# Spectral mixing and a gated bilinear layer: earlier direct weights at the block change, normalisation on two engines, and three low parts and a product group in another order

## The chip, the cores and the metric

The kernel runs on one core of a Trainium2 chip. The metric is the device time of one execution in microseconds (us); 727.72 us is the median of three runs of the kernel before, which lie between 727.48 and 728.47. TensorE is the matrix engine, VectorE (DVE), ScalarE (ACT) and GpSimd (POOL) are the other computing engines, and SyncE (SP) issues transfers. Each engine works through its own instructions in the order in which the program gives them; an instruction that waits holds everything behind it on the same engine.

## What is computed

The reference is a transformer-like block on 2048 tokens of 640 channels, in 32-bit floats:

```python
def _layernorm(x, axis=-1, eps=1e-5): ...
def _A_ref(x, w_r, w_i):                       # a filter in the frequency domain
    X = jnp.fft.rfft2(x, axes=(-2, -1))
    X = X * (w_r + 1j * w_i)
    return jnp.fft.irfft2(X, s=(S, D), axes=(-2, -1))
def _B_ref(x, w_gate, w_up, w_down):           # bilinear gate, F = 1728
    h = jnp.einsum("bsd,df->bsf", x, w_gate) * jnp.einsum("bsd,df->bsf", x, w_up)
    return jnp.einsum("bsf,fd->bsd", h, w_down)
h = x + _A_ref(_layernorm(x), w_r, w_i)
h2 = h + _B_ref(_layernorm(h), w_gate, w_up, w_down)
```

## The kernel before

**Stages.** The tokens are 16 tiles of 128 rows (tile t holds tokens t, t + 16, ...). First come the first layer norm and the forward transform (to about 115 us), then the inverse transform tile by tile: `id_mm`, `unfold` and `is1_mm` make the result of tile t and `acc` (L510) adds it to the rows `X[t]`. Tiles 8 to 15 are then written out to DRAM (the spill, L686), since their place in SBUF is wanted for something else. After that the bilinear layer runs in two blocks of eight tiles: block 0 (tiles 0 to 7), then block 1 (tiles 8 to 15).

**High and low parts.** The matrix products are done in a reduced 32-bit format. To keep accuracy, an operand is split into a high part (a copy in the reduced format, on ScalarE) and a low part (the operand less the high part, a subtraction on VectorE or GpSimd), and a product is three matmuls: high by high, high by low, low by high. `high_of` is L739, `low_of` L743; for weights it is `split_in` (L465 and L466) and `prep` (L706 to L723).

**The bilinear layer.** The 1728 gate columns are 14 pieces. Pieces 12 and 13 are done first in each block and directly (`p == 6` in the loop at the end: `gu` and `gate_parts`), with the direct weights that `load_direct` brings; pieces 0 to 11 are the chunks of a seven-product Strassen scheme (`strassen(c, ...)`, two chunks for each of the six steps p). A chunk computes into three PSUM banks, `p11`, `acc_a` and `p53`, out of four. In one chunk, in the order of the program: a product group into `acc_a`, copied by ScalarE (`p1`, L973); one into `p11`; a further one on `acc_a`, copied as `u2` (L987); one into `p53`, copied as `m5` (L995); one more on `acc_a`, added to `m5` on VectorE (L1002); one more on `p53`, to which `u2` is added (L1005). Then `h[0]` multiplies (L808), makes the high part on ScalarE and returns a function, `rest`, that makes the low part on VectorE. A last group on `acc_a` follows, and `h[1]` does the same with it. Between these stand the slots `at(0)` to `at(6)`, where work listed in `side` is put in; they come in the order 0, 1, 2, 3, 6, 4, 5.

**Down projection.** The gated results of a step are multiplied by the down weights during the next step, either as whole products (`down`, with `acc`) or, behind a "mixed" step, as 16 small stages (`mixed_down`, with the row additions at L917) that `tick` weaves between the matmul triples of the first chunk. Such a chunk is `woven`; `tick` also takes one function from the list `pending` (`flush(1)`). Steps 1 to 4 are mixed in block 0, steps 0 to 4 in block 1; step 5 (chunks 10 and 11) is not, but its chunk 10 is woven, as the step before it was mixed. In mixed chunks `rest` is an empty function.

**The block change.** In chunk 11 of block 0, `bring_back` (L731) loads the eight spilled tiles into the rows' old place; its first load waits for TensorE's last use of that place, in chunk 10. `load_direct` loads the direct weights of the next block: the 640 columns of `wlast` into a work buffer, and two halves of 640 columns into the staging tile `stage`. All eleven loads go to SyncE's queue. At slot 1 the weights are split (ScalarE L465, GpSimd L466) and the next raw weights are loaded. At slots 3, 6 and 5 `low` normalises tiles 8 to 15 (L527: scale and shift per row), on ScalarE. Block 1 then opens (`p == 6`): for each of the eight tiles, four transposes on TensorE (L539), copies on ScalarE (L549, L553) and subtractions on VectorE (L557), with a group of down products of block 0 (12 matmuls and one `acc`) after each tile but the first.

**The opening of block 0.** In the loop over the inverse transform, at t = 13 (`NT - 3`), new PSUM banks are opened and `gu(NC - 1, 0)` runs ahead of the products of tile 13. Later, in `p == 6` of block 0, `late()` is the low part of piece 12 (L658); it stands behind `t_rest` (eight subtractions), the t34 split and the low parts of the weights on VectorE.

Of the kernel before, what the change touches and what calls it, by code (L numbers as in the profile page):

```python
# [14 lines left out]
OP = mybir.AluOpType  # L15
# [31 lines left out]
def tile_spectral_glu(ctx: ExitStack, tc: tile.TileContext, x, wf, wgu, wlast, wdown, wdlast,  # L47
# [51 lines left out]
    def home(tag, shape, name, dt=F32):  # L99
        return keep.tile(shape, dt, tag=tag, name=name)  # L100
# [401 lines left out]
    def is1_mm(t):  # L502
        ps = PY[t] = pair("y")
        for b in range(2):
            mmx(ps[:, b, 0:320], cit, YT[t][:, 320 * b:320 * b + 320], True, True)
# [16 lines left out]
            SC[t] = r[:, i:i + 1], b[:, i:i + 1]  # L522
        return fs, cs

    def normalise(t, z):
        Z[t] = z
        act(z, X[t], AF.Identity, bias=SC[t][1], scale=SC[t][0])  # L527

    PT = {}
# [135 lines left out]
    for t in range(NT):  # L665
        for k in tside[t]:
            turn_mm(k)
        if t + 2 < NT:
            unfold(t + 2, dside[t], tside[t])
        else:  # L670
            for k in tside[t]:
                turn_hi(k)
                turn_lo(k)
        if t + 3 < NT:
            id_mm(t + 3)
        for f in aside[t]:
            f()
        if t == NT - 3:
            ht = home("qm", [P, 8192], "ht", F32R)
            hts, t3 = cut(ht, 0, 3, 2, 2, 512), cut(ht, 6144, 2, 2, 512)  # L680
            banks("a", "pglu")
            gu(NC - 1, 0)
        is1_mm(t)
        acc(t, PY[t], total[:, t:t + 1] if t < 8 else None)
        if t >= 8:
            nc.sync.dma_start(spill[t - 8], X[t])  # L686
        if t == NT - 2:
            late = gate_parts(NC - 1, 0, 0)
# [251 lines left out]
    def strassen(c, blk, h, ahead, downs, side, fine=()):  # L940
        wa, ws = W[c]
        fine = list(fine)

        def some(n):
            for _ in range(n):
                if downs:
                    downs.pop(0)()
                    pop(2)

        def at(n):  # L950
            if c == 1 and blk == 0:
                pop(5)
            for f in side.get(n, ()):
                f()

        def tick():
            if fine:
                fine.pop(0)()
                flush(1)

        b11, b21, b22 = ([operand(sb, k + i) for i in range(2)] for sb, k in ((0, 0), (0, 2), (1, 2)))
        t1, t2 = ([(TJ["12"][:, 0, m, k], TJ["12"][:, 1, m, k]) for k in range(2)] for m in range(2))
        t4 = [operand(1, k) for k in range(2)]
        b5 = [operand(sb, 4) for sb in range(2)]
        p11, acc_a, p53 = single(), single(), single()

        def product(o, w, a, ms, extra=(), start=True, tick=tick):
            triple(o, [(w, a + P * i, m) for i, m in enumerate(ms)] + list(extra), start, tick)

        woven = bool(fine)  # L970
        product(acc_a, wa, 384, b11, tick=None)
        p1, u2, m5 = (wk([P, 512], n) for n in ("p1", "u2", "m5"))
        act(p1, acc_a, AF.Copy)  # L973
        at(0)
        if not woven:
            flush(1)
        product(p11, wa, 0, b21, [(wa, 256, b5[0])])
        if ahead and not woven:
            ahead[0]()
            flush(2)  # L980
            ahead[1]()
            flush()
        if not woven:
            tt(p1, p11, p1, op=OP.add)
        at(1)
        product(acc_a, ws, 0, t2, start=False)
        act(u2, acc_a, AF.Copy)  # L987
        flush()
        if woven:
            tt(p1, p11, p1, op=OP.add)  # L990
        if ahead and woven:
            ahead[0]()
            ahead[1]()
        product(p53, ws, 256, t1, [(wa, 896, b5[1])])
        act(m5, p53, AF.Copy)  # L995
        if ahead and woven:
            ahead[2]()
            ahead[3]()
        some(2)
        at(2)  # L1000
        product(acc_a, ws, 640, [(t3[:, k, 0], t3[:, k, 1]) for k in range(2)], start=False)
        tt(m5, acc_a, m5, op=OP.add)  # L1002
        some(1)
        product(p53, ws, 896, b22, [(ws, 512, b5[1])], start=False)
        tt(p53, p53, u2, op=OP.add)  # L1005
        rest = h[0](p53, m5)
        at(3)
        some(2)
        rest()
        if ahead and not woven:  # L1010
            ahead[2]()
            ahead[3]()
        product(acc_a, wa, 640, t4, [(wa, 896, b5[0])], start=False)
        while fine:
            tick()
        some(1)
        at(6)
        rest = h[1](acc_a, p1)
        at(4)
        some(1)  # L1020
        rest()
        some(8)
        at(5)
# [5 lines left out]
    for n, (blk, p) in enumerate(steps):  # L1029
        if p == 6:  # L1030
            s13, s12 = count % 3, (count + 1) % 3
            if blk == 0:
                load_raw(0)
                copies, sums, high, low = prep(0, blk, nc.vector)
                TJ["12"] = home("qr", [P, 2, 2, 2, 512], "t12", F32R)
                t1s = [t12(j) for j in range(4)]
                for j in range(4):
                    t1s[j][0]()
                copies()
                t1s[0][1]()  # L1040
                late()
                t1s[1][1]()
                t1s[2][1]()
                fifth((5, 6, 7))
                t1s[3][1]()
                late = gate_parts(NC - 2, 0, s12)
                sums()
                high()
                for j in range(4):
                    t_rest(j)  # L1050
                hi, lo = t34(0)
                hi()
                low()
                lo()
                late()
                gu(NC - 1, 1)
                wdn = load_d(p)
                gate_parts(NC - 1, 1, s13)()
            else:
                copies, sums, high, low = prep(0, blk)  # L1060
                js = [4, 5, 6, 7, 0, 1, 2, 3]
                for j in range(8):
                    transp(8 + j)
                    if j % 4 == 3:
                        fifth(range(5 + j, 9 + j))
                    if j >= 1:
                        down(*prev, js[j - 1], True)
                    if j == 3:
                        copies()
                        sums()  # L1070
                high()
                low()
                down(*prev, js[7], True)
                gu(NC - 1, 0)
                gate_parts(NC - 1, 0, s13)()
                gu(NC - 2, 0)
                TJ["12"] = home("qr", [P, 2, 2, 2, 512], "t12", F32R)
                t1s = [t12(j) for j in range(4)]
                late = gate_parts(NC - 2, 0, s12)
                for j in range(4):  # L1080
                    t1s[j][0]()
                    t_rest(j)
                late()
                gu(NC - 1, 1)
                for j in range(4):
                    t1s[j][1]()
                wdn = load_d(p)
                late = gate_parts(NC - 1, 1, s13)
                hi, lo = t34(0)
                hi()  # L1090
                late()
                lo()
            gu(NC - 2, 1)
            gate_parts(NC - 2, 1, s12)()
            first_wd = wdn
            prev = (blk, 6, [(2 * k, 2 * k + 1) for k in (s12, s13)])
            count += 2
            load_raw(1)
            if blk == 0:
                fs, cs = scale_shift(range(8, 16), None)  # L1100
                fill.extend(fs + cs)
            continue
# [15 lines left out]
        for ci in range(2):  # L1118
# [11 lines left out]
            elif ci == 0:  # L1130
                side[3] = [lambda wdn=wdn: issue(wdn)]
            if c == 11 and blk == 0:
                bring_back()
                dj = load_direct(1, [wk([P, D], "draw"), stage[:, 0:640], stage[:, 640:1280]])
                side[1] = [lambda: issue(dj[0]), lambda: issue(dj[1]), lambda: load_raw(0)]

                def low(ks):
                    for k in ks:
                        if k == 0:
                            TJ["z"] = home("qr", [P, 6, D], "zt")  # L1140
                        normalise(8 + k, TJ["z"][:, k] if k < 6 else wk([P, D], "z"))

                side[3] = [lambda: low(range(4))]
                side[6] = [lambda: low((4, 5))]
                side[5] = [lambda: low((6, 7))]
            strassen(c, blk, hs[ci], ahead, downs if ci == 0 else [], side, fine if ci == 0 else ())
            count += 1
        prev = (blk, p, units)
# [134 lines left out]
```

## Time and profile before

| | |
|---|---|
| median of three runs | 727.72 us |
| profiled execution, its own time | 726.67 us |
| its span in the profile | 724.9 us |
| mean granted TensorE clock | 0.99 |
| TensorE busy in 423.0 to 429.4 us | 0.00 of 6.40 us |
| idle time of TensorE that ends at L987, VectorE's L658, L496 | 6.6, 1.2, 1.1 us |

A line of the timeline reads: start, length (both us), engine, source line, operation, what it writes and reads, shape, count, and in brackets how long the engine had been idle and whose work ended that. Where a line merges several instructions, the length goes from the first's start to the last's end. PE is TensorE's matmul row, PEld its weight loads, which run beside the matmuls. L82 is the helper that all matmuls of the later stages go through, so those are told apart by tile names: `e` are the chunk's banks, `y` the banks of the down products.

### The profile page before, as it was taken

The page shows a single profiled execution, that of the slowest core. Times are in us where ns is not written, and L with a number is a line of the kernel's source. Part 1 is how long each engine was busy: PE and PEld are TensorE (multiplying, and loading weights), DVE is VectorE, ACT ScalarE, POOL GpSimd, SP SyncE. Part 2 cuts the span into 40 slices and gives each one's busy share as a digit, 9 for nine tenths or more (in the row PEclk, how much of TensorE's full clock was granted, in tenths as well). Part 3 has the DMA queues.
Part 4 walks back from the last instruction along what each step waited for, and adds up shares of the span by engine and source line. Part 5 has one row for each costly group of instructions (what it writes and reads, how often), then busy time and mean ns, then how long its engine had stood idle before and what let it go on. Part 6 is the DMA issues. An engine that isn't in the chain of part 4 may idle for free.

```text
span 724.9 us, 10120 instructions
## 1 busy us (share of the span) xinstructions
PE 694.0 (96%) x3784; PEld 607.1 (84%) x3784; DVE 477.9 (66%) x839; ACT 305.5 (42%) x574; POOL 367.0 (51%) x342
## 2 busy tenths in 40 slices
PE   7999998999999999999999967999999999999998
PEld 6788997987878898888888846989888888888887
DVE  7968887897968446666666615565565757565654
ACT  4756666365533323433334227252434252433320
POOL 3301114332155585959596621219678686868610
PEclk9999999999999999999999989999999999999999
DMA  9405765002321212121111061320030302020203
GB/s 337 166 1 174 233 213 168 1 20 81 118 74 37 72 37 73 38 73 37 58 51 38 36 234 38 128 90 26 14 108 0 110 1 103 6 79 32 72 1 146
DMA packets 23234, 60.30 MB, mean 83 GB/s; under 512 B 2577, under 2 KB 7185, under 8 KB 23185
## 3 DMA queue, kind: packets, MB, share of 16 engines
q1 hardware_dynamic: 22608, 57.94, 23.2%
q0 software_dynamic: 288, 1.48, 0.6%
q8 instruction: 30, 0.49, 0.3%
q10 hardware_dynamic: 288, 0.23, 0.1%
q14 instruction: 20, 0.16, 0.1%
HBM read 51.78 MB, written 7.86 MB: 82 GB/s over the span
## 4 chain that ended last, share of the span: by engine, by line
PE 77%; DVE 12%; issue 4%; DMA 4%; ACT 2%; POOL 0%; SPq 0%; DVEq 0%; POOLq 0%; ACTq 0%
PE e L82 41%; PE y L82 24%; PE re L82 2%; PE im L82 2%; PE u L343 2%; PE eo L82 2%; DMA raw<-in_wgu_dram 2%; DVE fold L193 1%; DVE fold L198 1%; PE im L393 1%; PE im L392 1%; PE ir L384 1%; DVE ex L743 1%; DMA x<-in_x_dram 1%; DVE xb L917 1%
## 5 line engine op out<-in xcount | busy, mean ns | idle before, releaser
L82 PE MATMUL e<-xt,wst 128*128 128x512 f32 x864 | 220.4, 393 | 1.3 <-DVE ht L658 1.2
L82 PEld LDWEIGHTS e<-xt,wst 128*128 128x128 f32 x864 | 158.6, 189 | 29.8 <-DVE ht L658 1.6
L82 PE MATMUL y<-wd,ht 128*128 128x320 f32 x880 | 152.4, 312 | 2.4 <-DVE x L510 1.0
L82 PEld LDWEIGHTS y<-wd,ht 128*128 128x128 f32 x880 | 139.9, 190 | 14.9 <-DVE x L510 1.3
L707 POOL TENSOR_TENSOR wst<-raw,wst 128x1024 fp32r<-128x1024 f32 x24 | 57.6, 2402 | 96.9 <-ACT wst L706 96.6
L82 PE MATMUL e<-t,wst 128*128 128x512 f32 x288 | 74.1, 391 | 0.0
L723 POOL TENSOR_TENSOR wst<-raw,wst 128x896 fp32r<-128x896 f32 (+1 forms) x46 | 65.1, 1436 | 9.7 <-ACT wst L718 9.7
L739 ACT ACTIVATE ht<-e 128x512 fp32r<-128x512 f32 x48 | 27.6, 596 | 92.9 <-DVE e L808 47.2
L917 DVE TENSOR_TENSOR xb<-y,xb 128x640 f32<-128x640 f32 x60 | 49.4, 824 | 26.0 <-PE y L82 24.2
L82 PEld LDWEIGHTS e<-t,wst 128*128 128x128 f32 x288 | 52.6, 188 | 8.6
L917 DVE TENSOR_TENSOR x<-y,x 128x640 f32<-128x640 f32 x48 | 39.5, 824 | 20.9 <-PE y L82 20.0
L1002 DVE TENSOR_TENSOR m<-e,m 128x512 f32<-128x512 f32 x24 | 16.5, 687 | 54.7 <-PE e L82 54.6
L743 DVE TENSOR_TENSOR ht<-e,ht 128x512 fp32r<-128x512 f32 x48 | 33.1, 689 | 23.1 <-ACT ht L739 22.6
L82 PE MATMUL e<-ht,wst 128*128 128x512 f32 x144 | 39.8, 403 | 6.6 <-ACT u L987 6.6
L718 ACT ACTIVATE wst<-raw 128x896 fp32r<-128x896 f32 (+1 forms) x48 | 30.1, 677 | 32.2 <-POOL raw L712 31.4
L82 PE MATMUL y<-ex,ht 128*128 128x320 f32 x216 | 43.4, 309 | 0.0
L82 PE MATMUL e<-xt,wdir 128*128 128x512 f32 x180 | 41.9, 392 | 1.1 <-DVE q L496 1.1
L466 POOL TENSOR_TENSOR wd<-draw,wd 128x640 fp32r<-128x640 f32 x10 | 16.3, 1653 | 49.6 <-ACT wd L465 49.6
L510 DVE TENSOR_TENSOR x<-y,x 128x640 f32<-128x640 f32 x32 | 26.2, 820 | 21.7 <-PE y L82 21.7
L82 PEld LDWEIGHTS e<-xt,wdir 128*128 128x128 f32 x180 | 33.4, 188 | 8.3 <-ACT xt L549 1.3
L411 POOL CAST qr<-bits 1x128 fp32r<-1x128 f32 x16 | 4.5, 280 | 68.0 <-DVE qr L408 68.0
L82 PEld LDWEIGHTS y<-ex,ht 128*128 128x128 f32 x216 | 36.2, 188 | 3.2
(212 smaller groups left out, 1302.8 us busy)
## 6 DMA issues: line engine op xcount, KB each, us to landing
raw<-in_wgu_dram SPq DMA_DIRECT2D x24, 640.0 KB, 3.9
wts<-in_wf_dram SPq DMA_DIRECT2D x16, 644.0 KB, 4.0
draw<-in_wdown_dram SPq DMA_DIRECT2D x24, 320.0 KB, 4.6
x<-in_x_dram SPq DMA_DIRECT2D x16, 320.5 KB, 5.9
bits<-in_mm_dram SPq DMA_DIRECT2D x32, 128.0 KB, 3.9
sp<-x SPq DMA_DIRECT2D x8, 320.0 KB, 2.1
xb<-sp SPq DMA_DIRECT2D x8, 320.0 KB, 5.3
out_dram<-x SPq DMA_DIRECT2D x8, 320.0 KB, 2.2
```

The costliest lines, as they stand in the source:

```text
L82: nc.tensor.matmul(o, l, r, start=start, stop=stop, skip_group_check=True)
L193: lambda: nc.vector.scalar_tensor_tensor(view(f, 320, [[161, 2], [1, 161]]), view(XP[t], 0, [[320, 2], [1, 161]]), SC[t][1], view(XP[t], 6 ...
L343: nc.tensor.matmul(ps[h][:, 0:NQ], WM[g][0][:, h], T[g][:, h], start=True, stop=True)
L466: los.append(lambda r=r, a=a, b=b: engine.tensor_tensor(w[:, 1, a:b], r, f32(w[:, 0, a:b]), op=OP.subtract))
L510: tt(xv, ps[:, :, 0:320], xv, op=OP.add)
L707: nc.gpsimd.tensor_tensor(wa[:, 1], stage[:, 0:1024], f32(wa[:, 0]), op=OP.subtract)
L718: act(ws[:, 0, o:o + b - a], stage[:, a:b], AF.Copy)
L723: ptt(ws[:, 1, o:o + b - a], stage[:, a:b], f32(ws[:, 0, o:o + b - a]), op=OP.subtract)
L739: act(unit(u)[0], src, AF.Copy)
L743: engine.tensor_tensor(lo, src, f32(hi), op=OP.subtract)
L917: tt(xv, PQ[q][:, :, 0:320], xv, op=OP.add)
L1002: tt(m5, acc_a, m5, op=OP.add)
```

## The change

Five edits. At the block change the three weight loads are issued ahead of the eight row loads; tiles 8 to 11 are normalised on ScalarE at slot 2 (before: slot 3), tiles 12 and 13 on VectorE at slot 3 and tiles 14 and 15 on VectorE at slot 6. In woven chunks `rest` of `h[0]` is put into `pending`, so that it comes out behind the next stage of `mixed_down`. At t = 13 the products and the addition of tile 13 come ahead of the new banks and `gu(NC - 1, 0)`. In the opening of block 0 `late()` comes ahead of `t_rest`.

```diff
-    def normalise(t, z):
+    def normalise(t, z, vector=False):
         Z[t] = z
+        if vector:
+            nc.vector.tensor_scalar(z, X[t], SC[t][0], SC[t][1], op0=OP.mult, op1=OP.add)
+            return
         act(z, X[t], AF.Identity, bias=SC[t][1], scale=SC[t][0])
...
         if t == NT - 3:
+            is1_mm(t)
+            acc(t, PY[t])
             ht = home("qm", [P, 8192], "ht", F32R)
             hts, t3 = cut(ht, 0, 3, 2, 2, 512), cut(ht, 6144, 2, 2, 512)
             banks("a", "pglu")
             gu(NC - 1, 0)
-        is1_mm(t)
-        acc(t, PY[t], total[:, t:t + 1] if t < 8 else None)
+        if t != NT - 3:
+            is1_mm(t)
+            acc(t, PY[t], total[:, t:t + 1] if t < 8 else None)
...
         some(2)
-        rest()
+        if woven:
+            pending.append(rest)
+        else:
+            rest()
...
                 high()
+                late()
                 for j in range(4):
                     t_rest(j)
                 hi, lo = t34(0)
                 hi()
                 low()
                 lo()
-                late()
                 gu(NC - 1, 1)
...
             if c == 11 and blk == 0:
+                dj = load_direct(1, [wk([P, D], "draw"), stage[:, 0:640], stage[:, 640:1280]])
                 bring_back()
-                dj = load_direct(1, [wk([P, D], "draw"), stage[:, 0:640], stage[:, 640:1280]])
                 side[1] = [lambda: issue(dj[0]), lambda: issue(dj[1]), lambda: load_raw(0)]
...
-                        normalise(8 + k, TJ["z"][:, k] if k < 6 else wk([P, D], "z"))
-
-                side[3] = [lambda: low(range(4))]
-                side[6] = [lambda: low((4, 5))]
-                side[5] = [lambda: low((6, 7))]
+                        normalise(8 + k, TJ["z"][:, k] if k < 6 else wk([P, D], "z"), k > 3)
+
+                side[2] = [lambda: low(range(4))]
+                side[3] = [lambda: low((4, 5))]
+                side[6] = [lambda: low((6, 7))]
```

## The prediction

> **What bounds the kernel now.** I read the page first, then the table of waits of TensorE, then the timeline around the waits that the change could touch, and the windows for the granted clock.
>
> ```profile
> span 724.9 us, 10120 instructions
> PE 694.0 (96%) x3784; PEld 607.1 (84%) x3784; DVE 477.9 (66%) x839; ACT 305.5 (42%) x574; POOL 367.0 (51%) x342
> ```
>
> TensorE is busy for 96% of the span; 31 us are idle. The waits of TensorE name what ends its idle time (columns: total, times, longest):
>
> ```profile
> PE e L82 <- ACT u L987: 6.6, 1, 6.6
> ...
> PE y L82 <- DVE xb L917: 0.6, 1, 0.6
> PE y L82 <- DVE x L917: 0.5, 1, 0.5
> ```
>
> The first is in the change from token block 0 to block 1, by far the longest single wait of the kernel; the two others are in chunk 10 of each block. The timeline around the switch, in order:
>
> ```profile
> 407.01 2.83 POOL L723 TENSOR_TENSOR wst<-raw,wst 128x896 fp32r<-128x896 f32 x2 [0.24 <-ACT wst L718]
> ...
> 415.81 3.62 PE L82 MATMUL e<-xt,wst 128*128 128x512 f32 x15
> 416.00 3.80 SPq L736 DMA_DIRECT2D xb<-sp  x8
> ...
> 420.65 1.08 SPq L464 DMA_DIRECT2D raw<-in_wgu_dram  x2
> ...
> 427.41 1.50 ACT L465 ACTIVATE wdir<-raw 128x640 fp32r<-128x640 f32 x2
> 428.81 0.58 ACT L987 ACTIVATE u<-e 128x512 f32<-128x512 f32 x1
> ...
> 432.17 5.18 PE L82 MATMUL e<-xt,wst 128*128 128x512 f32 x18
> ...
> 437.30 4.97 ACT L527 ACTIVATE zt<-xb,b,r 128x640 f32<-128x640 f32 x6
> ...
> 441.69 2.00 PE L82 MATMUL y<-wd,ht 128*128 128x320 f32 x12
> ...
> 444.28 0.58 ACT L549 ACTIVATE xt<-e 128x512 fp32r<-128x512 f32 x1
> ...
> 447.82 3.53 PE L82 MATMUL y<-wd,ht 128*128 128x320 f32 x12 [1.04 <-DVE x L510]
> ...
> 453.37 0.60 PE L539 MATMUL e<-ident,zt 128*128 128x128 f32 x4
> ```
>
> Chunk 11 starts at 415.81. SyncE issues eight row loads (L736) and only then the direct weights (L464). ScalarE splits these (L465) ahead of L987 in its own order, and L987 empties the bank that TensorE needs. So 6.6 us of TensorE hang on a transfer that stood behind 2.6 MB of rows. The windows show a second cost (columns: window, length, busy times, granted clock, DMA share, GB/s):
>
> ```profile
> 429.40:432.40 3.00, 2.96 (x7) 2.38 (x8) 0.00 (x0) 0.48 (x1) 2.56 (x2) 0.50 0.00 0
> 442.00:446.00 4.00, 2.19 (x16) 1.84 (x14) 1.32 (x2) 4.00 (x8) 0.00 (x0) 1.00 0.00 0
> 446.00:450.00 4.00, 2.84 (x12) 2.60 (x13) 3.73 (x7) 3.69 (x7) 0.18 (x1) 0.72 0.22 86
> ```
>
> After the gap the granted clock was 0.50, and it fell again, to 0.72, behind the thinly filled stretch from 442. Chunk 11 of block 1 is the same chunk with nothing in its way:
>
> ```profile
> 694.46 3.60 PE L82 MATMUL e<-xt,wst 128*128 128x512 f32 x15
> ...
> 696.90 0.69 DVE L743 TENSOR_TENSOR ht<-e,ht 128x512 fp32r<-128x512 f32 x1 [0.81 <-ACT ht L739]
> ...
> 699.52 0.60 ACT L987 ACTIVATE u<-e 128x512 f32<-128x512 f32 x1 [2.23 <-PE e L82]
> ...
> 704.90 0.70 DVE L1005 TENSOR_TENSOR e<-e,u 128x512 f32<-128x512 f32 x1 [1.29 <-PE e L82]
> ...
> 706.74 14.82 PE L82 MATMUL y<-wd,ht 128*128 128x320 f32 x96
> 707.00 0.69 DVE L743 TENSOR_TENSOR ht<-e,ht 128x512 fp32r<-128x512 f32 x1 [0.67 <-ACT ht L739]
> ...
> 708.33 0.60 ACT L739 ACTIVATE ht<-e 128x512 fp32r<-128x512 f32 x1 [1.36 <-DVE e L808]
> ```
>
> It takes 706.74 - 694.46 = 12.28 us; in block 0 it takes 432.17 + 5.18 - 415.81 = 21.54 us. That pair is the core of the forecast.
>
> **Part 1, the deferred low part in chunk 10 (both blocks).**
>
> ```profile
> 413.35 0.69 DVE L743 TENSOR_TENSOR ht<-e,ht 128x512 fp32r<-128x512 f32 x1 [0.73 <-ACT ht L739]
> 413.96 1.55 DVE L917 TENSOR_TENSOR x<-y,x 128x640 f32<-128x640 f32 x2
> ```
>
> VectorE stands 0.73 us for ScalarE's high part, then does the low part, then the row addition that TensorE waits for (0.5 us in block 0, 0.6 in block 1). With the low part behind the first addition, that addition starts at about 412.6 and ends 0.82 later, before TensorE asks at 414.28 (its 414.83 start less the wait). Gain 0.55 in each block. Late next: the low part, 0.1 us later than before; its bank is wanted only in chunk 11's third product, some 5 us on, so nothing. In mixed chunks the deferred function is empty. Bounds: 0 (if another addition of the pair is awaited) to 0.6 each.
>
> **Part 2, direct weights first.** The load of the wlast half waits only for a free buffer; the two raw halves wait for their staging tile, whose last reader is GpSimd's L723, done at 407.01 + 2.83 = 409.84.
>
> ```profile
> SPq L736 <- PE y L82: 17.7, 1, 17.7
> ...
> draw<-in_wdown_dram SPq DMA_DIRECT2D x24, 320.0 KB, 4.6
> ...
> DMA to landing us min/median/max: 2.9/5.3/6.5
> ```
>
> SyncE reached the row loads 17.7 us before 416.0, so it will be free for the weights; a 320 KB load lands in 4.6 us (page), hence about 414.5, before chunk 11 starts. The rows (last line: their times to landing) still wait for TensorE's last read of their home and issue as before, less the 0.55: 415.45 to 418.7, landed by 425.2 at the latest. ScalarE then splits the weights right behind its first copy of the chunk: three at 1.50 / 2 = 0.75 take 2.25 us, and in block 1 ScalarE sits idle for 2.23 us just there. L987 is wanted at chunk start + (699.52 - 694.46) = 5.06 us, 420.3, and comes on time; if it is late, TensorE still has nine matmuls (2.2 us) before it needs the bank. So chunk 11 runs from 415.26 to 427.54.
>
> **Part 3, normalisation.** Four stay on ScalarE, behind the m5 copy. That copy follows L987's place by nine matmuls of 0.24 (415.81: 15 in 3.62), so it starts at 422.5, and the four, 4.97 / 6 = 0.83 each, run from 423.1 to 426.4, with rows 0 to 3 landed one by one from about 421. The high part needs ScalarE only after L808, at 427.1 (chunk start + 10.44 for L1005, and two operations of 0.7). Four go to VectorE: two behind L808 and ahead of the low part, two ahead of the last L808. Behind them on VectorE wait the low part and the last product, then ScalarE's last high part, and behind that the first copy of the turned tokens, L549 (444.28 before). The trace has no such operation on VectorE with 640 columns. Its nearest rows:
>
> ```profile
> L217 DVE TENSOR_SCALAR bits<-cct,r x15: 276/279/754, 10.8 to 45.7; 128x128 f32<-128x128 f32 x15
> L466 DVE TENSOR_TENSOR wdir<-raw,wdir x3: 1371/1374/1378, 138.7 to 145.4; 128x640 fp32r<-128x640 f32 x3
> L141 DVE TENSOR_SCALAR ve<-mv 128x2 f32<-128x2 f32 x1 | 0.2, 160 | 0.0
> ```
>
> From 2 to 128 columns the same operation grows by 119 ns, 0.94 ns a column; 640 columns give 279 + 512 x 0.94 = 0.76 us. Bounds: 0.52 (half that slope) and 1.37 (the slowest 640-column row of VectorE). I take 0.76, the same kind of instruction. [...]
>
> In block 1 the last high part starts 708.33 - 694.46 = 13.87 us after the chunk, with VectorE idle 0.67 of that behind L808; the first two normalisations fill this. So: 415.26 + 13.87 - 0.67 + 4 x 0.76 = 431.5, and L549 follows at 432.0 instead of 444.28. From L549 to the third group of down products it was 447.82 - 444.28 = 3.54 us, a chain of copies and additions that the change leaves alone: 435.5. TensorE's own work up to there, two groups of down products (2.00) and five of transposes (0.60), would let it start at 427.54 + 7.0 = 434.5, so the chain decides, by 1.0 us. These 12 matmuls took 3.53 us at the low clock and 2.00 at the full one (441.69). Before, only transposes ran from 443.69 to 447.82, 4.1 us; now that stretch is 2.2 us (433.3 to 435.5). I take the full clock: done at 437.5 instead of 451.35. **Gain of the switch, chunk 10 of block 0 included: 13.8 us.** From there on TensorE set the pace before, and every later input (the next raw load, GpSimd's sums) has moved along.
>
> **Part 4, the opening of block 0.**
>
> ```profile
> 174.31 3.68 PE L82 MATMUL e<-xt,wdir 128*128 128x512 f32 x15 [1.12 <-DVE q L496]
> 177.83 1.24 PE L82 MATMUL y<-yt,tab 128*128 128x320 f32 x4
> ...
> 201.22 4.02 PE L82 MATMUL e<-xt,wst 128*128 128x512 f32 x15 [1.20 <-DVE ht L658]
> 202.29 0.58 ACT L655 ACTIVATE u<-e 128x512 f32<-128x512 f32 x1
> 202.92 1.90 PEld L82 LDWEIGHTS e<-xt,wst 128*128 128x128 f32 x9 [0.47 <-ACT u L655]
> ```
>
> The inverse-transform products of tile 13 (about 1.1 us) move into the 1.12 us in which TensorE waits; the gate products start 0.2 later and everything behind comes 0.9 earlier. VectorE's addition of tile 13, the last spill and the raw load queued behind it on SyncE move along, so I carry 0.85 us to 202.9. The L658 edit lets the first six products start up to 1.2 us earlier, but the next nine wait for the bank that L655 frees at 202.9, which stands on ScalarE behind VectorE work whose sum doesn't change. Gain of L658: 0 (bounds 0 and 1.2).
>
> **Sum.** 13.8 + 0.55 + 0.85 = 15.2 us, off the profiled execution's 726.67: 711.5. The median of the runs is 1.05 above that execution; so 712.5.
>
> **The rivals.**
> (a) *VectorE at double rate*, 0.52 us or less: four times 0.24 saved, where TensorE's own work would stop it too: 711.5. Against it the slope of L217. [...] 15%.
> (b) *The clock falls again*, because the switch is still thin: 3.53 - 2.00 = 1.5 us lost, 714.0. For it: 446 to 450, 0.72 after a window that was over half busy. [...] 12%.
> (c) *VectorE becomes the bound*: 1.37 us each adds 4 x 0.61 = 2.4, 714.9; the rows landing 2.5 us late would do the same. 12%.
> (d) *The weights don't come early*, because SyncE is held at a buffer that frees late. Up to about 418 it costs nothing; if they still share the wires with the rows, the 6.6 us gap stays and only parts 1, 4 and an L549 some 2.4 us earlier remain: 727.7 - 1.1 - 0.85 - 2.4 = 723.4. 5%.
> (e) *Slower: the bank order turns.* A chunk takes three of four banks in the order in which they come free. If the earlier L658 turns this order, the first product of a chunk gets the bank that the chunk before frees last, by a low part that ends 3.1 us after the chunk starts (block 1: 696.90 + 0.69 against 694.46). It decides from six of the 22 chunk boundaries on (18.6 us against 15.2); at all 22, 68.2 - 15.2 = 53 us slower, 781. Against it: that bank is released before any chunk takes one, and no other release passes it. 2%.
>
> **How the numbers follow.** Forecast 54% at 712.5; (a) 15, (b) 12, (c) 12, (d) 5, (e) 2. The range goes from 710.3 ((a) with L658's whole 1.2) to 716.4 ((b) and (c) together), and leaves out (d) and (e). 0.2% of the time, 1.5 us, is what a measurement of this kernel can tell from nothing: faster 0.96, same 0.02, slower 0.02.
>
> **What would show it.** Right: no wait of TensorE for L987; L736 issued behind L464 and still near 415.5; the chunk before the switch 12.3 us long; L549 near 432; clock 1.00 throughout 420 to 450; both L917 waits and L496's gone, L655 in the place of L658. Wrong: L465 waiting for a DMA, ScalarE idle at L527, a wait on L743 or L510 of more than 1 us after 430, or a clock below 1 behind 435.

## The result, and the profile after

| | before | after |
|---|---|---|
| median | 727.60 us (4 runs, 727.36 to 728.47) | 709.79 us (4 runs, 709.61 to 710.23) |
| profiled execution, its own time | 726.67 us | 709.82 us |
| span | 724.9 us | 708.0 us |
| mean granted clock | 0.99 | 0.996 |

The ratio is 0.9754, with a 95% interval of 0.9737 to 0.9771: 17.8 us faster. The forecast was 712.5 us, 15.2 us of gain; the result lies 2.7 us below it and 0.5 us below the low end of the range. Between the two profiled executions the gain is 16.85 us. So there are two questions: why the profiled execution gained 1.65 us more than 15.2, and why the median gained 1.0 us more than the profiled execution.

The page's first lines, of after:

```profile
span 708.0 us, 10116 instructions
PE 689.5 (97%) x3784; PEld 605.8 (86%) x3784; DVE 479.4 (68%) x843; ACT 302.4 (43%) x570; POOL 367.6 (52%) x342
```

TensorE is now idle for 18.5 us instead of 31; it is also busy for 4.5 us less with as many matmuls, since fewer ran at a low clock (three groups at the switch took 1.52 us for 2.93, 4.25 for 5.18 and 2.02 for 3.53; the window below). Four instructions went from ScalarE to VectorE. The waits of TensorE, after:

```profile
PE e L82 <- ACT u L658: 1.4, 1, 1.4
PE y L82 <- DVE x L510: 1.4, 2, 1.1
```

The wait for u2 (L987, now L993) is gone, those for the row additions (L917, now L923) too. The first line is the bank in the opening that the forecast named as the next in the way (L655, now L658; L661 is what was L658). The timeline at the block change, after:

```profile
408.71 0.80 SPq L464 DMA_DIRECT2D raw<-in_wgu_dram  x2
...
413.95 3.61 PE L82 MATMUL e<-xt,wst 128*128 128x512 f32 x15
414.14 3.85 SPq L742 DMA_DIRECT2D xb<-sp  x8
...
417.30 1.37 ACT L465 ACTIVATE wdir<-raw 128x640 fp32r<-128x640 f32 x2
...
418.96 0.60 ACT L993 ACTIVATE u<-e 128x512 f32<-128x512 f32 x1 [0.30 <-PE e L82]
...
421.55 3.35 ACT L530 ACTIVATE zt<-xb,b,r 128x640 f32<-128x640 f32 x4
...
422.16 4.25 PE L82 MATMUL e<-xt,wst 128*128 128x512 f32 x18
...
425.74 1.13 DVE L528 TENSOR_SCALAR zt<-xb,r,b 128x640 f32<-128x640 f32 x2
...
427.39 1.13 DVE L528 TENSOR_SCALAR z<-xb,r,b 128x640 f32<-128x640 f32 x2
...
429.23 2.00 PE L82 MATMUL y<-wd,ht 128*128 128x320 f32 x12
...
429.65 0.59 ACT L552 ACTIVATE xt<-e 128x512 fp32r<-128x512 f32 x1
...
433.22 2.02 PE L82 MATMUL y<-wd,ht 128*128 128x320 f32 x12 [1.05 <-DVE x L510]
...
442.46 3.77 PE L82 MATMUL y<-wd,ht 128*128 128x320 f32 x24
```

The weights are issued at 408.7, ahead of the rows at 414.1. ScalarE splits them by 418.7, and u2 follows at 418.96, waiting only for its own product. Chunk 11 runs from 413.95 to 426.41, 12.46 us instead of 21.54. The first copy of the turned tokens (L552, before L549) comes 15.70 us after the chunk's start instead of 28.47. The third group of down products starts 3.57 us behind it and takes 2.02 us. The last pair of groups stands at 442.46; before, it stood at 458.55. The clock around the third group, in a window of after (columns as in the prediction):

```profile
432.40:436.00 3.60, 2.78 (x20) 2.77 (x21) 3.60 (x7) 2.98 (x6) 0.77 (x1) 1.00 0.43 162
```

The clock (third number from the end) is 1.00 here. Before, it was 0.72 in the window of the same group (446 to 450) and 0.50 behind the wait for u2. The opening of block 0, after:

```profile
173.31 1.31 PE L82 MATMUL y<-yt,tab 128*128 128x320 f32 x4 [0.32 <-DVE x L510]
...
174.22 3.82 PE L82 MATMUL e<-xt,wdir 128*128 128x512 f32 x15
...
198.83 1.52 PE L82 MATMUL e<-xt,wst 128*128 128x512 f32 x6
...
201.79 2.34 PE L82 MATMUL e<-xt,wst 128*128 128x512 f32 x9 [1.44 <-ACT u L658]
...
203.97 2.91 PE L82 MATMUL e<-t,wst 128*128 128x512 f32 x12
```

The products of tile 13 now come first, behind a wait of 0.32 us, and the gate products start without one. The six products that waited for VectorE (L658 before) start at once, and the next nine wait 1.44 us instead. The group at 203.97 stood at 205.08 before: 1.1 us, of which 0.2 was there already at 169 us, ahead of every edit.

### The profile page after: what moved, and what is told of

Read it like the earlier page. It is cut to its first block, busy times and chain, and to the rows that moved or that the text cites. A ratio compares the mean times of both kernels' runs of the same rounds, so it can differ in the third digit from the quotient of the medians.

```text
span 708.0 us, 10116 instructions
## 1 busy us (share of the span) xinstructions
PE 689.5 (97%) x3784; PEld 605.8 (86%) x3784; DVE 479.4 (68%) x843; ACT 302.4 (43%) x570; POOL 367.6 (52%) x342
## 4 chain that ended last, share of the span: by engine, by line
PE 80%; DVE 13%; issue 5%; DMA 1%; ACT 1%; POOL 0%; DVEq 0%; SPq 0%; POOLq 0%; ACTq 0%
PE e L82 43%; PE y L82 25%; PE re L82 2%; PE im L82 2%; PE u L343 2%; PE eo L82 2%; DVE fold L193 1%; DVE fold L198 1%; PE im L392 1%; PE im L393 1%; PE ir L384 1%; DVE ex L749 1%; DVE x L512 1%; DMA raw<-in_wgu_dram 1%; DVE bits L217 1%
## 5 line engine op out<-in xcount | busy, mean ns | idle before, releaser
L82 PE MATMUL y<-wd,ht 128*128 128x320 f32 x880 | 150.8, 309 | 1.3 <-DVE x L510 1.1
L923 DVE TENSOR_TENSOR xb<-y,xb 128x640 f32<-128x640 f32 x60 | 49.5, 824 | 26.0 <-PE y L82 24.2
L923 DVE TENSOR_TENSOR x<-y,x 128x640 f32<-128x640 f32 x48 | 39.6, 824 | 20.8 <-PE y L82 19.9
L749 DVE TENSOR_TENSOR ht<-e,ht 128x512 fp32r<-128x512 f32 x48 | 33.0, 688 | 17.8 <-ACT ht L745 17.3
L879 ACT ACTIVATE wd<-draw 128x640 fp32r<-128x640 f32 x18 | 13.3, 740 | 58.7 <-POOL draw L892 48.1
```

The costliest lines, as they stand in the source:

```text
L82: nc.tensor.matmul(o, l, r, start=start, stop=stop, skip_group_check=True)
L749: engine.tensor_tensor(lo, src, f32(hi), op=OP.subtract)
L879: act(w[:, 0, a:b], r, AF.Copy)
L923: tt(xv, PQ[q][:, :, 0:320], xv, op=OP.add)
```

## The experiments

Three theories are set against each other. *Theory*: the parts give what the prediction says of each, and the rest comes from the low clock behind the thin stretch of the switch. *Rival 1*: the weights give little by themselves, as the wait would return at the rows. *Rival 2*: sharing the normalisation between two engines is what pays. The medians and ratios below are against the kernel before, measured beside each on the same chip (727.3 to 727.7 us, 17 to 21 runs). Differences from the kernel after are differences of medians that were not measured side by side; four runs of one kernel can lie 2 us apart, so differences of some tenths of a us rest on the traces.

### The parts alone

**Weights first, alone** (e1_weights).

```diff
-                bring_back()
                 dj = load_direct(1, [wk([P, D], "draw"), stage[:, 0:640], stage[:, 640:1280]])
+                bring_back()
```

> Only the three weight loads ahead of the row loads. Theory (transfer order): no wait of TensorE for L987, chunk 11 takes 12.3 us instead of 21.5; the eight normalisations stay on ScalarE at their old slots, so the first copy of turned tokens (L549) comes only some 8 us after the chunk's end; 9.0 us faster, up to 10.5 if the clock stays at 1.00 behind it. Rival (the gain is the moved normalisation, the transfers only shift the wait to the rows): a wait of ScalarE for the rows takes the place of the wait for the weights, at most 3 us faster.

Measured 718.15 us (716.03 to 720.56, 4 runs), ratio 0.9872 (0.9851 to 0.9893): 9.2 us. The timeline of this kernel:

```profile
417.53 3.62 PE L82 MATMUL e<-xt,wst 128*128 128x512 f32 x15
...
425.75 4.24 PE L82 MATMUL e<-xt,wst 128*128 128x512 f32 x18
...
436.93 0.59 ACT L549 ACTIVATE xt<-e 128x512 fp32r<-128x512 f32 x1
...
440.46 3.57 PE L82 MATMUL y<-wd,ht 128*128 128x320 f32 x12 [1.04 <-DVE x L510]
...
443.83 1.05 PE L539 MATMUL e<-ident,zt 128*128 128x128 f32 x4
...
444.54 2.82 PE L82 MATMUL y<-wd,ht 128*128 128x320 f32 x12
```

Chunk 11 takes 12.46 us (425.75 + 4.24 - 417.53), as in after, so the reordered loads alone remove the wait, and rival 1 falls. But L549 is still 19.40 us behind the chunk's start, and behind the long stretch the third group takes 3.57 us, the transposes 1.05 instead of 0.60 and the fourth group 2.82 instead of 2.00; the granted clock was 0.50 in 440 to 445. The times of its runs are up to 4.5 us apart.

**Normalisation alone** (e2_norm): the edits to `normalise` and to the slots.

> Only the normalisations moved to slots 2, 3 and 6, four of them on VectorE; the weights still come behind the rows. Theory: the wait of 6.6 us for L987 and the low clock behind it stay, L549 comes about 3.7 us earlier; 3.7 us faster, up to 5.2 if the clock no longer falls at the switch. If this and the run with the weights alone add up to less than the 14.3 us that the switch gained in the changed kernel, the rest is the clock. Rival (all from the order of transfers): no change.

Measured 722.98 us (722.12 to 723.67, 4 runs), ratio 0.9936 (0.9924 to 0.9949): 4.3 us. A wait and a timeline row of this kernel:

```profile
PE e L82 <- ACT u L990: 7.1, 1, 7.1
```

```profile
446.22 2.03 PE L82 MATMUL y<-wd,ht 128*128 128x320 f32 x12 [1.05 <-DVE x L510]
```

The wait for u2 stays. The third group takes 2.03 us at a granted clock of 1.00 (445 to 450), behind a thin stretch of 2.0 us (444.24 to 446.22): this half is worth its earlier L549 and the clock behind it.

**Part 1 alone** (e3_rest): `rest` goes into `pending`.

> Only the deferred low part in woven chunks. The prediction's step: 0.55 us in each block, 1.1 us faster together. Theory after the result: 0.8 us in each block, 1.6 us faster, because the stop of TensorE also costs the weight load that can't run beside a matmul when the products start again.

Measured 725.79 us (724.99 to 728.16, 8 runs), ratio 0.9974 (0.9964 to 0.9984): 1.5 us, more than the 1.1 of the prediction. The section on why the prediction was wrong shows where the difference lies.

**Tile 13 alone** (e4_tile13), **L658's place alone** (e5_late).

```diff
         if t == NT - 3:
+            is1_mm(t)
+            acc(t, PY[t])
...
                 high()
+                late()
                 for j in range(4):
                     t_rest(j)
...
-                late()
```

> Only the products and the addition of tile 13 ahead of the gate products. The prediction's step: 0.85 us faster, with the wait at L658 (1.2 us) still there. Rival (VectorE's work behind it sets the start of chunk 0): no change.

> Only the low part of piece 12 (L658) ahead of the eight subtractions in the opening of block 0. The prediction's step: no change (within 0.3 us), as the second product group of chunk 0 waits for ScalarE's L655 until 202.9 either way. Rival: the 1.2 us that TensorE waited for L658 are gained.

Measured 726.53 us (12 runs), ratio 0.9992 (0.9983 to 1.0001), and 727.02 us (11 runs), ratio 0.9995 (0.9986 to 1.0003). The first is 0.8 us by the medians, but its interval just takes in no change; L496 is no longer among its long waits. The second is no change, as the prediction's zero for that edit said: its trace shows 1.4 us of TensorE at L655 in the place of the 1.2 at L658.

The five alone add up to 9.2 + 4.3 + 1.5 + 0.8 + 0.5 = 16.3 us, against 17.8 together. The last two can't be told from nothing, and the interval of the first alone reaches 1.5 us to either side, so this doesn't show that the parts gain by acting together. The traces point the same way. From the start of chunk 11 to the last pair of groups it takes 42.74 us before, 34.86 with the weights alone, 38.05 with the normalisation alone and 28.51 in after: 7.9 and 4.7 us, against 14.2. But the thin stretch cost 2.8 us in the profile of the weights alone and 1.5 in that of before, and the wait for u2 was 7.1 us with the normalisation alone and 6.6 before: 1.8 us together, about as much as is missing. Both sizes vary between executions of one kernel, as the next section shows.

### What the kernel before does from run to run

**The kernel before once more** (e6_before_again), with no edit.

> The kernel before once more, unchanged, for the spread of its executions. Theory: its executions differ by up to 1 us because the clock falls and rises again at the switch at a moment that differs from run to run, so its spans scatter around 725 to 726.5 and its mean clock with them, and the changed kernel (no such fall) scatters less than half as much; the profiled 726.67 was one of the shortest. Rival: taking the profile moves the time, then all executions without one lie within 0.3 us of 727.6.

Measured 727.68 us (726.84 to 728.83, 11 runs, spans of 725.0 to 727.1), ratio 1.0005 (0.9995 to 1.0015). Its profiled execution took 727.97 us, 1.30 more than the one behind the prediction. The timeline of this second profile:

```profile
415.69 3.62 PE L82 MATMUL e<-xt,wst 128*128 128x512 f32 x15
...
447.91 3.57 PE L82 MATMUL y<-wd,ht 128*128 128x320 f32 x12 [1.03 <-DVE x L510]
...
451.28 1.05 PE L539 MATMUL e<-ident,zt 128*128 128x128 f32 x4
...
451.99 2.89 PE L82 MATMUL y<-wd,ht 128*128 128x320 f32 x12
...
459.90 3.76 PE L82 MATMUL y<-wd,ht 128*128 128x320 f32 x24
```

From the start of chunk 11 to the last pair of groups it takes 459.90 - 415.69 = 44.21 us; in the first profile it was 458.55 - 415.81 = 42.74. Of the 1.47 us between them 1.4 are here: the low clock lasted through the transposes (1.05 for 0.60) and the fourth group (2.89 for 2.00) as well. So one kernel pays 1.5 us for the thin stretch in one execution and 2.9 in another. The profile behind the prediction had caught the cheaper case, which is also the commoner one in the traces: the three profiles that leave the switch as it was (part 1 alone, tile 13 alone, L658's place alone) pay 1.4, 1.5 and 1.7 us.

The thin stretch is not the only source of scatter. The wait for u2 is 6.6 us in the first profile and 7.5 in the second. And the clock fell in other places too. In the profiles of the weights, the normalisation and part 1 alone it was 0.50 from about 125.5 to 129 us, where it is 1.00 in the first profile; in the last of them this cost 1.6 us. In that of part 1 alone, at 728.16 us the longest of its eight runs, the clock fell once more, in the opening of block 0 (a row of the timeline, then a window):

```profile
203.57 5.29 PE L82 MATMUL e<-xt,wst 128*128 128x512 f32 x15 [1.93 <-DVE ht L658]
...
204.00:207.50 3.50, 3.50 (x10) 2.73 (x9) 2.09 (x4) 2.48 (x5) 0.00 (x0) 0.52 0.78 317
```

The same 15 matmuls take 4.02 us in the first profile, behind a wait of 1.20.

### The size of the normalisation, and the clock

**Every VectorE normalisation done twice** (e7_twice), on top of after.

```diff
-            nc.vector.tensor_scalar(z, X[t], SC[t][0], SC[t][1], op0=OP.mult, op1=OP.add)
+            for _ in range(2):
+                nc.vector.tensor_scalar(z, X[t], SC[t][0], SC[t][1], op0=OP.mult, op1=OP.add)
```

> The changed kernel, with each of the four normalisations on VectorE done twice (same result). Theory: VectorE's row is what sets the first copy of turned tokens (L549) and with it the third group of down products, so four more at 0.53 us come out in full: 2.1 us slower than the changed kernel. Rival (TensorE's own work sets that group, which by the prediction it could start 1.0 us earlier): 1.1 us slower or less.

Measured 715.19 us (715.10 to 715.37, 4 runs), ratio 0.9831 (0.9818 to 0.9845): 5.4 us over after, not the 2.1 expected. Its timeline:

```profile
426.02 2.43 DVE L529 TENSOR_SCALAR zt<-xb,r,b 128x640 f32<-128x640 f32 x4
...
429.87 2.01 PE L82 MATMUL y<-wd,ht 128*128 128x320 f32 x12
...
432.53 0.59 ACT L553 ACTIVATE xt<-e 128x512 fp32r<-128x512 f32 x1
...
436.10 3.57 PE L82 MATMUL y<-wd,ht 128*128 128x320 f32 x12 [1.05 <-DVE x L510]
```

Four more normalisations put the first copy 2.6 us later (18.30 us after the chunk's start at 414.23, against 15.70), so VectorE is on the path and each costs about 0.65. The other 2.8 us are the clock, 0.50 in 435 to 440 and 0.82 in 440 to 445: 429.87 + 2.01 to 436.10 is a stretch of 4.2 us with transposes and waits alone, and the group behind it takes 3.57 us, as in the second profile of the kernel before.

**The same, with 12 matmuls more** (e9_twice_filled), and **the same 12 in the kernel before** (e10_before_filled): one group of down products of the switch is computed twice, the second time from the start.

```diff
-        for n, (l, r) in enumerate(seq):
-            for b in range(2):
-                mmx(ps[:, b, 0:320], l, r[:, 320 * b:320 * b + 320], n == 0, n == len(seq) - 1)
+        for _ in range(2 if last and blk == 0 and j == 5 else 1):
+            for n, (l, r) in enumerate(seq):
+                for b in range(2):
+                    mmx(ps[:, b, 0:320], l, r[:, 320 * b:320 * b + 320], n == 0, n == len(seq) - 1)
```

> The kernel with the doubled normalisations, with the second group of down products at the switch (tile 5) computed twice into its own bank (same result): 12 more matmuls, 2.0 us of TensorE, put just ahead of the stretch of 4.2 us in which TensorE does nothing but transposes. Theory (a stretch of transposes without products makes the clock fall, and the fall costs 2.8 us there): the stretch shrinks to about 2.2 us, the clock stays at 1.00, and more work makes the kernel faster, 715.2 to about 712.5 us. Rival (the fall comes from the waits, or the work is paid for): the same 715.2 or up to 2 us slower.

> The same 12 additional matmuls in the kernel before. Theory: the second fall of the clock (behind 442 us) goes away, the one behind the 6.6 us wait stays; 1.5 to 2.9 us faster, about 2.4 in the median, and the executions scatter less than those of the kernel before (726.1 to 728.8). Rival: no change or slower, same scatter.

Measured 712.42 us (712.23 to 713.73, 4 runs), ratio 0.9792 (0.9780 to 0.9805), 2.8 less than without them; and 725.84 us (725.08 to 727.81, 12 runs), ratio to before 0.9977 (0.9969 to 0.9986), 1.85 us less. Timelines of the one and of the other:

```profile
429.53 3.77 PE L82 MATMUL y<-wd,ht 128*128 128x320 f32 x24
...
435.77 2.03 PE L82 MATMUL y<-wd,ht 128*128 128x320 f32 x12 [1.05 <-DVE x L510]
```

```profile
441.68 3.77 PE L82 MATMUL y<-wd,ht 128*128 128x320 f32 x24
...
447.80 2.02 PE L82 MATMUL y<-wd,ht 128*128 128x320 f32 x12 [1.03 <-DVE x L510]
```

The group of 24 fills the thin stretch down to about 2.4 us; the next group starts where it would have started, with the same wait, and takes 2.0 instead of 3.6 us. Twelve matmuls of no use make both kernels faster. This isolates the clock: nothing else in the order of the two kernels was changed. In the kernel before the gain is smaller than the 2.4 us expected, and the other half of the expectation failed: the runs scatter as much as before (725.08 to 727.81, against 726.49 to 728.90), though ten of the twelve lie within 1.0 us. So the thin stretch makes only a part of that scatter.

**All eight on ScalarE, at the new slots** (e8_allact).

```diff
-                        normalise(8 + k, ..., k > 3)
+                        normalise(8 + k, ..., False)
```

> The changed kernel, with all eight normalisations on ScalarE at the new slots. Theory: four more at 0.83 us stand ahead of ScalarE's last high part and first copy instead of four at 0.53 us on VectorE, but ScalarE is idle for part of that time: L549 between 0 and 1.2 us later, 0 to 1.2 us slower than the changed kernel. Rival (sharing is what pays): 2.5 us slower or more, with the clock falling behind the longer thin stretch.

Measured 710.03 us (709.88 to 711.95, 4 runs), ratio 0.9766 (0.9753 to 0.9780), 0.24 over after. Its timeline:

```profile
429.91 0.58 ACT L552 ACTIVATE xt<-e 128x512 fp32r<-128x512 f32 x1
...
433.46 2.03 PE L82 MATMUL y<-wd,ht 128*128 128x320 f32 x12 [1.05 <-DVE x L510]
```

The first copy comes 16.14 us after the chunk's start at 413.77, 0.44 later than in after. So rival 2 falls: what pays is the earlier slots, and the second engine is worth about 0.4 us in the trace (0.2 by the medians, which is within their noise).

**Each VectorE normalisation as two of 320 columns** (e11_halves).

```diff
-            nc.vector.tensor_scalar(z, X[t], SC[t][0], SC[t][1], op0=OP.mult, op1=OP.add)
+            for a in (0, 320):
+                nc.vector.tensor_scalar(z[:, a:a + 320], X[t][:, a:a + 320], SC[t][0], SC[t][1], op0=OP.mult, op1=OP.add)
```

> The changed kernel, with each normalisation on VectorE as two of 320 columns. [...] Time: the four more fixed parts lie on the path to L549, about 0.2 us each: 0.8 us slower than the changed kernel, more if the clock falls.

Measured 711.34 us (710.27 to 712.55, 4 runs), ratio 0.9774 (0.9760 to 0.9788). The line's instructions, of after and then of this kernel (least, median and largest ns):

```profile
L528 DVE TENSOR_SCALAR zt<-xb,r,b x2: 604/607/610, 425.7 to 426.3; 128x640 f32<-128x640 f32 x2
```

```profile
L529 DVE TENSOR_SCALAR zt<-xb,r,b x4: 436/443/444, 425.4 to 426.5; 128x320 f32<-128x320 f32 x4
```

From 320 to 640 columns the operation grows by 607 - 443 = 164 ns, 0.51 ns a column; carried on to no columns, this leaves 0.28 us, an estimate. The 0.2 us for each of the four more fixed parts was an estimate of the author's that no run had shown. Here the third group comes 20.04 us after the chunk's start (433.68 - 413.64) instead of 19.27 (433.22 - 413.95): 0.77 later, 0.19 for each of the four. Two of the four runs, at a mean clock of 1.00, took 710.3 us; the other two, at 0.993, about 712.5. The profile is one of the faster two; behind a thin stretch of 2.7 us (430.94 to 433.68) its third group took 2.02 us. Where the clock fell in the slower two is open: they have no trace.

### A faster version

**The next two waits of after taken out** (e12_better): in the opening, the low part of the t34 split goes behind the multiplication of the gate, so that VectorE reaches the latter earlier; in the switch, the addition of a finished group of down products goes ahead of the copies of the tile that was turned last.

```diff
-                lo()
                 gu(NC - 1, 1)
                 wdn = load_d(p)
-                gate_parts(NC - 1, 1, s13)()
+                end = gate_parts(NC - 1, 1, s13)
+                lo()
+                end()
...
-                    transp(8 + j)
+                    turn_mm(8 + j)
+                    if j in (1, 2):
+                        down(*prev, js[j - 1], True)
+                    turn_hi(8 + j)
+                    turn_lo(8 + j)
                     if j % 4 == 3:
                         fifth(range(5 + j, 9 + j))
-                    if j >= 1:
+                    if j > 2:
                         down(*prev, js[j - 1], True)
```

> The changed kernel with two more moves. In the opening of block 0 the low part of t34 (1.2 us on VectorE) goes behind the multiplication of piece 13, so that ScalarE's L658 and the second product group of chunk 0 come earlier: the wait of 1.4 us there shrinks to about 0.3. At the switch the addition of a finished group of down products goes ahead of the copies of the tile turned last, so that the third group finds its bank: the wait of 1.05 us goes. Theory: 2.0 us faster than the changed kernel, 707.8. Rival (something else is late at once in both places): no change.

Measured 708.63 us (708.38 to 709.94, 4 runs), ratio to before 0.9740 (0.9728 to 0.9753): 1.2 us less than after by the medians and 1.4 by the profiled executions, where 2.0 was expected; the intervals of the two ratios overlap. Its timeline:

```profile
201.02 2.34 PE L82 MATMUL e<-xt,wst 128*128 128x512 f32 x9 [0.47 <-ACT u L658]
...
203.48 3.02 PE L82 MATMUL e<-t,wst 128*128 128x512 f32 x12
...
413.42 3.61 PE L82 MATMUL e<-xt,wst 128*128 128x512 f32 x15
...
431.71 2.03 PE L82 MATMUL y<-wd,ht 128*128 128x320 f32 x12
```

In the switch the third group comes 18.29 us after the chunk's start instead of 19.27 and no longer waits for L510: the 1.0 us hoped for. In the opening the wait for L658 fell from 1.44 to 0.47, but the group behind it stands only 0.5 us earlier (203.48 against 203.97). It now waits for ScalarE's L979, which stands behind L660, and that behind VectorE's L659; and L659 comes only 0.27 us earlier, at 201.63 for 201.90, since the low part of the split and then L665 stand ahead of it.

## Why the prediction was wrong, point by point

**The step that failed** is the last one of the sum: "The median of the runs is 1.05 above that execution; so 712.5." It adds the distance between one profiled execution and the median of before to the forecast for after. In after the profiled execution (709.82) and the median (709.79) are 0.03 us apart, so 1.1 of the 2.7 us come from this step.

Where the distance comes from is shown in part. The forecast priced the low clock behind the thin stretch at 1.53 us, from one execution; the second profile of before, 1.30 us longer, pays 2.9 for it, and the change removes the stretch. But with that stretch filled in the kernel before (e10_before_filled), the profiled execution (725.26) and the median (725.84) are still 0.58 us apart. So, by one profiled execution of each, the stretch explains about half of the distance, and the rest stays open; the other falls of the clock and the varying wait for u2 are candidates. Nor do four runs of after, within 0.6 us, show that its runs scatter less: those of all eight on ScalarE lie 2.1 apart, those of the faster version 1.6.

The other 1.65 us are terms that were mis-sized:
- **VectorE's normalisation**, 0.76 us each: measured 0.61 long and 0.53 apart, as two take 1.13. Four times 0.23 is 0.92, and L552 comes 15.70 us after the chunk's start instead of 16.74 (432.0 - 415.26). The slope between the 2 columns of L141 and the 128 of L217, 0.94 ns, was the wrong one to carry to 640: between 320 and 640 it is 0.51. Rival (a) reckoned with half of 0.94 and was nearly right on the slope (0.47 for 0.51), and at 0.53 from start to start nearly on the price (0.52 or less). That VectorE works at a double rate, as (a) is called, was not shown; the run with halves shows the slope alone.
- **Part 1**, 0.55 us a block: measured 0.80. The rows of chunk 10, before and then after:

```profile
413.41 0.87 PE L82 MATMUL e<-xt,wst 128*128 128x512 f32 x3
414.83 0.71 PE L82 MATMUL y<-wd,ht 128*128 128x320 f32 x3 [0.55 <-DVE x L917]
415.37 0.60 PE L82 MATMUL y<-ex,ht 128*128 128x320 f32 x3
```

```profile
412.35 0.87 PE L82 MATMUL e<-xt,wst 128*128 128x512 f32 x3
413.06 0.61 PE L82 MATMUL y<-wd,ht 128*128 128x320 f32 x3
413.51 0.60 PE L82 MATMUL y<-ex,ht 128*128 128x320 f32 x3
```

Without a wait the next group starts 0.71 us after the one that is shown 0.87 long: groups overlap at their ends. With the wait it is 1.42 us, 0.71 more and not 0.55, and the next one follows 0.09 later behind the group after the stop (415.37 - 414.83 against 413.51 - 413.06). Behind the stop the group's weight loads start together with its matmuls (414.83), without it 0.23 us ahead of them (412.83 and 413.06). That is 0.80 a block, twice 0.25 over the forecast; part 1 alone measured 1.5 us.
- What remains, 0.2 us, is as much as the two profiled executions were already apart at 169 us, ahead of every edit.

**The steps that held.** The wait for u2 left whole, and chunk 11 takes 12.46 us where 12.28 was forecast. The row loads were issued as before relative to TensorE (414.14, 0.19 behind the chunk's start), so bringing the weights past them cost nothing. Nothing waited for the four on ScalarE. The chain from L552 to the third group took 3.57 us (3.54), and the clock stayed at 1.00. That the chain and not TensorE's own work decided, by 1.05 us (1.0), is in part luck: the two groups and five sets of transposes ahead took 5.76 us (426.41 to 432.17) and not the 7.0 that the forecast got by adding their lengths, and the chain came as much earlier by the faster normalisations. Tile 13 gave 0.9 us in the trace (0.85). The earlier L658 gave nothing, with L655's wait in its place, as the run of it alone showed.

**The rivals.** (b), another clock fall, did not come true in after, whose stretch is 2.0 us (429.23 + 2.00 to 433.22), but did in the kernel with doubled normalisations, whose stretch is 2.2 us longer. At the switch the third group took 3.2 to 3.6 us behind stretches of 4.1 to 4.2 us (seven profiles) and 2.0 behind 1.0 to 2.7 (seven). In the opening of block 0, with part 1 alone, the clock was 0.52 behind a wait of only 1.93 us. (c) fell as a size: VectorE does set L552 (the doubled work cost 2.6 us in full), but at 0.53 each. (d) fell with the weights alone. (e) fell: no wait of a chunk's first product appears.

## What to carry to other kernels

Price a gap of TensorE twice, by the wait and by the clock behind it, and take the clock's price from several executions, since it varied between two of one kernel (1.5 and 2.9 us behind the same stretch). Don't carry the distance between a profiled execution and the median over to the changed kernel without knowing what makes it. Price a stop inside a stream of matmuls from start to start and not by the idle time shown: in chunk 10 it cost 0.71 us that way, where 0.55 was shown. Before work is shared between engines, try it at the better place in the order on the engine that has it: here that was all but about 0.4 us of what the normalisation's edit brought.

## What the runs showed of the hardware

- A stretch of 4.1 to 4.2 us that holds only transposes and waits is followed by a group of 3.2 to 3.6 us instead of 2.0, in all seven profiles that have it; matmuls ran slowly for 3.4 (part 1 alone) to 7.0 us (the second profile of before) from there. In the seven in which it is 1.0 to 2.7 us long, that group took 2.0. But the length alone does not decide: in the profile of part 1 alone the clock was 0.52 (204.0 to 207.5) behind a wait of 1.93 us in the opening of block 0, a place ahead of which 45 matmuls take 10.48 us without a stop in the first profile of before. What share the transposes have in a fall was not shown, as no run here held transposes without waits.
- Twelve useless matmuls in such a stretch, 1.8 us of TensorE, saved 2.8 us in one kernel and 1.85 in another.
- A tensor_scalar on VectorE with two scalars per row took 0.61 us for 640 columns and 0.44 for 320, with 0.53 from start to start of the longer ones; the same operation on ScalarE took 0.83 (six in 4.97).
